# Sigmoid attention with a ReGLU layer behind it: three weight sums, two relus and two token sums change their places in the order

## The chip, the cores and the metric

The kernel runs on one core of a Trainium2 chip. The metric is the device time of one execution in microseconds (us). A core has four compute engines with an instruction stream each: TensorE (PE, with its weight loads PEld), VectorE (DVE), ScalarE (ACT) and GpSimd (POOL). SyncE (SP) and POOL issue most DMAs. Each engine works its stream in order; streams wait for each other by semaphores.

## The reference

Eight batches of 12 heads with 448 tokens of 64 channels. Attention has a sigmoid in place of the softmax; its output, 3584 tokens of 768 channels, goes through a gated layer:

```python
scores = scale * np.matmul(q, k.transpose(0, 1, 3, 2)) - np.log(S)
attn = 1.0 / (1.0 + np.exp(-scores))
x = matmul(attn, v)                      # then (batch, token, head*64)
gate = np.maximum(x @ w_gate, 0.0)       # 768 -> 1536
out = (gate * (x @ w_val)) @ w_out       # 1536 -> 768
```

Inputs and output are float32; the kernel multiplies in float16 and adds up in float32.

## The kernel before, in words

**Attention.** A batch has three groups of four heads. q and k are transposed: batches 0 and 1 on TensorE (`pe_transposes`), later ones by DMA (`dma_transposes`, L218): VectorE copies k and q into a `rel` buffer (L222, two buffers, L53), and SP issues one DMA transpose of it (L226). `qk_unit` (L299) makes the scores of one of seven key chunks of a group in two PSUM banks, and ScalarE writes their sigmoids into `PT` (L187). `pv` (L249) multiplies the seven chunks by v into two banks, which `put_xT` copies into `xT` (L184).

**PSUM.** After the first stage all eight banks are one ring: `bank` (L77) takes the one in front and puts it at the back. So each tile takes the bank of the tile eight places before it, and its first matmul waits until that tile has been read.

**The gated layer.** `gv` (L311) does one block f of 128 of the 1536 columns for some tokens: six matmuls for the gate product `g_ps`, six for the value product `v_ps`, then in `gv_out` (L331) a relu into `gate_sb` (on ScalarE, L334, if `act_relu`, otherwise on VectorE, L336) and on VectorE the product `hT` = gate times value (L343), here called the gating. The gating frees the bank of `v_ps`, the relu that of `g_ps`. For batch 0 a block is done in two halves of tokens, 256 (half 0) and 192 (half 1), called units. For batch 1 the blocks 8 to 11 are done whole (kind "u" in `work`); its other blocks and all of the later batches go by a seven-product scheme (`gv_split`, `gv_pair`), and so do most of the down products (`down_pair`, L460). Those schemes want sums of blocks, made by VectorE beforehand: `early_sum_steps` (L563: four steps for two blocks, 0 to 7, one `gate_sums` in place in wv and three S tiles), `weight_sums` (L410: the four T tiles, sums of blocks of wo) and `token_sum_steps` (L440: four sums of `hT`; only the first two are moved here).

**The order around the first edit.** It is written out by hand. In batch 1 the 21 qk units come in six stretches, `cuts` (L933): in the fourth and sixth, pv of a group stands after two qk units. After each stretch `ffn_mix` (L770) takes 4, 3, 3, 3, 3 and 4 units of batch 0 from `gv_queue`, which `push_first` has filled in the order half 0, half 1 for each pair of blocks. The fifth stretch has the units (half 0, f 9), (half 1, f 8) and (half 1, f 9). Hooks run before a unit: in the fifth stretch the k and q copies and the transpose of batch 2's group 0 before the first unit and of group 1 before the third, in the sixth `late_loads` before the first. `late_loads` (L868) does the copies and transpose of group 2, then `hold` (L861): POOL copies two numbers of that group's transposed tile, so that every POOL DMA behind it (v of batch 2, k and q of batch 3, the two loads of wo, v of batch 3) is issued after that transpose has landed. `given` (L953) says how many sum steps VectorE gets at each unit.

**The order around the second edit.** Batches 2 and on have again six stretches, each followed by one item of `work` (`next_work`, L901); `ahead` jobs run before the item, `jobs` beside it. In batch 2 the fifth stretch's item is block 10 of batch 1, the sixth's is block 11, and batch 3's first is the first down pair, `("y", 0, 0)`. `open_late` (L383) opens the T tiles and the pool of S tiles. Before the fifth item comes weight sum 0 = a difference of two quarters of wo, before the sixth weight sum 1, the first token sum and the copies of batch 3's group 2; beside it the other three token sums.

Of the kernel before, what the change touches and what calls it, by code (L numbers as in the profile page):

```python
# [18 lines left out]
def kernel(  # L19
# [170 lines left out]
    def qkT_of(b, g):  # L190
        if (b, g) not in qkT_tiles:
            qkT_tiles[(b, g)] = qkTp.tile([P, TW, P], FP16, tag="qkT", name="qkT")
        return qkT_tiles[(b, g)]
# [24 lines left out]
    def dma_transposes(b, g):  # L218
        k16, q16, _ = in_tiles[b]
        rel = relp.tile([P, TW, P], FP16, tag="rel", name="rel")  # L220
        for ti, t16 in enumerate((k16, q16)):
            nc.vector.tensor_copy(  # L222
                rel[:, ti * NCH : (ti + 1) * NCH, :].rearrange("p c (h d) -> p h c d", h=2),
                t16[:, 2 * g : 2 * g + 2, :].rearrange("p h (c d) -> p h c d", c=NCH),
            )
        nc.sync.dma_start_transpose(  # L226
            qkT_of(b, g)[:], rel[:].rearrange("p c x -> p (c x)")
        )
# [78 lines left out]
    def pv_group(b, g):  # L307
        pv(b, g, 0, S, [PT_tiles.pop((b, g, c))[:, :, 0:S] for c in range(NCH)])
# [81 lines left out]
    def sub(o, a, b):  # L390
        nc.vector.tensor_tensor(out=o, in0=a, in1=b, op=AOP.subtract)  # L391

    def sums_tile(inner):
        S3 = late["sums"].tile([P, 3, HF * P], FP16, tag="S", name="S")
        return [S3[:, i, :].rearrange("p (x y) -> p x y", y=inner) for i in range(3)]
# [14 lines left out]
    def weight_sums(i):  # L410
        T = [late["T"][:, j] for j in range(4)]
        B11, B21 = wo[:, 0:HF, 0:HM], wo[:, HF:NFC, 0:HM]
        B12, B22 = wo[:, 0:HF, HM:DM], wo[:, HF:NFC, HM:DM]
        sub(T[i], *((B12, B11), (B22, T[0]), (B22, B12), (B21, T[1]))[i])
# [14 lines left out]
    def token_blocks(g, p):  # L429
        blocks = []  # L430
        for gt, t in tiles_in(g, p):
            h = odd[gt] if gt < g else hT_tiles[g][:, :, t * P : (t + 1) * P]
            blocks += [h[:, 0:HF, :], h[:, HF:NFC, :]]
        return blocks
# [5 lines left out]
    def token_sum_steps(g, p, k0=0, k1=HF):  # L440
        if ("y", g, p) not in sums:
            sums[("y", g, p)] = sums_tile(P)
        S1, S2, S4 = (t[:, k0:k1, :] for t in sums[("y", g, p)])
        A11, A12, A21, A22 = (t[:, k0:k1, :] for t in token_blocks(g, p))
        return (
            lambda: nc.vector.tensor_tensor(out=S1, in0=A21, in1=A22, op=AOP.add),
            lambda: sub(S2, S1, A11),
            lambda: sub(S4, A12, S2),
            lambda: sub(A21, A11, A21),
        )  # L450
# [311 lines left out]
    def push_gv(b, q0, qn, fs, act_relu=True):  # L762
        for f in fs:
            gv_queue.append(lambda f=f: gv(b, q0, qn, f, act_relu))

    def push_first(half, fs, act_relu=True):
        c0, c1 = HALVES[half]
        push_gv(0, 64 * c0, 64 * (c1 - c0), fs, act_relu)

    def ffn_mix(count, hooks=(), steps=(), given=()):  # L770
        hooks = list(hooks)
        for left in range(count, -1, -1):
            while hooks and hooks[0][0] >= left:
                hooks.pop(0)[1]()
            if left:
                gv_queue.popleft()()
                for step in itertools.islice(steps, given[count - left] if steps else 0):
                    step()


    nc.scalar.activation(gate[:], zeros[:, 0:2], AF.Sigmoid, bias=sig_bias, scale=qk_scale)
# [3 lines left out]
    half = QCUT // 2 * D  # L785
# [61 lines left out]
    push_first(1, range(0, 4))  # L847
    for f0 in range(4, 12, 2):
        for half in range(2):
            push_first(half, range(f0, f0 + 2))  # L850


    order = [(g, c) for g in range(NG) for c in range(NCH)]
# [1 line left out]
    def pv_finish(b):  # L855
        pv_group(b, NG - 1)
# [7 lines left out]
    def both(b, g):  # L864
        pe_transposes(b, g, 0)
        pe_transposes(b, g, 1)
# [64 lines left out]
    for b in range(1, B):  # L931
        if b == 1:
            cuts, pv_at = (0, 3, 6, 9, 13, 17, 21), {3: (0, 2), 5: (1, 2)}  # L933
        else:
            cuts, pv_at = (0, 4, 7, 11, 14, 18, 21), {0: (-1, 2), 2: (0, 2), 4: (1, 2)}
        bursts = list(range(len(cuts) - 1))
        inner = {}
        if b > 2:
            inner = {0: 1, 3: 5} if b == 3 else {0: 1} if b % 2 == 0 else {2: 3, 3: 5} if b == B - 1 else {4: 5}
            for n in inner.values():  # L940
                bursts.remove(n)
        count = len(bursts)
        hooks = {}
        if b == 1:
            mix = (4, 3, 3, 3, 3, 4)
            hooks = {
                1: [(3, lambda: both(1, 1))],
                3: [(3, lambda: both(1, 2))],
                4: [(3, lambda: dma_transposes(2, 0)), (1, lambda: dma_transposes(2, 1))],
                5: [(4, late_loads)],  # L950
            }
            steps = itertools.chain.from_iterable(early_sum_steps(j, 2 * j) for j in range(4))
            given = ((0, 1, 1, 0), (1, 1, 0), (1, 1, 1), (1, 1, 0), (2, 1, 0), (1, 1, 1, 1))  # L953
        else:
            mix = (0,) * count

        def burst(n):
            for i, (g, c) in enumerate(order[cuts[n] : cuts[n + 1]]):
                if n in pv_at and i == pv_at[n][1]:
                    if n == 0:  # L960
                        pv_finish(b - 1)
                        if b == 2:
                            push_group(0)
                        elif b % 2 == 0:
                            push_group(b // 2 - 1)
                    else:
                        pv_group(b, pv_at[n][0])
                qk_unit(b, g, c)

        for m in range(count):  # L970
            jobs, ahead = [], []
            burst(bursts[m])
            if m == 0 and b > 3:
                jobs.append(lambda: dma_transposes(b, 2))
            if b == 2 and m == 2:
                ahead.append(lambda: dma_transposes(3, 0))
            elif b == 2 and m == 3:
                jobs.append(lambda: dma_transposes(3, 1))
            elif b == 3 and m == count - 1:
                jobs.append(lambda: dma_transposes(4, 1))  # L980
            elif 0 <= m - count + 2 and 3 < b < B - 1:
                jobs.append(lambda: dma_transposes(b + 1, m - count + 2))
            if b == 1:
                if m == 0:
                    load(2, 0, 1, "kq")
                    load(2, 1, 2, "kq")
                    load(2, 2, 3, "kq")
            elif m == 0 and b + 1 < B:
                for g0, g1 in ((0, 1), (1, NG)) if b == 3 else ((0, NG),) if b > 3 else ():
                    jobs.append(lambda g0=g0, g1=g1: load(b + 1, g0, g1, "kq"))  # L990
                jobs.append(lambda: load_v(b + 1))
            if b == 2 and m == 0:
                ahead.append(lambda: split_sums(1))
            elif b == 2 and m == 4:
                open_late()
                ahead.append(lambda: weight_sums(0))
                first_sums = token_sum_steps(0, 0)
            elif b == 2 and m == 5:
                ahead += [lambda: weight_sums(1), first_sums[0], lambda: dma_transposes(3, 2)]
                jobs += first_sums[1:]  # L1000
            elif b == 3 and m == 0:
                jobs.append(lambda: (weight_sums(2), weight_sums(3)))
            elif b == 3 and m < 3:
                jobs.append(lambda: gate_sums(6 + 2 * m, 8 + 2 * m))
            if b % 2 and b > 2:
                if m == count - 1:
                    jobs.append(lambda: (batch_sums_t1(b // 2), batch_sums(b // 2, (0, 1))))
            elif b > 3 and m == 0:
                jobs.append(lambda: batch_sums(b // 2 - 1, (1, HD)))
            if mix[m]:  # L1010
                for job in jobs:
                    job()
                ffn_mix(mix[m], hooks.get(m, ()), steps, given[m])
            else:
                next_work(
                    jobs, ahead=ahead,
                    amid=(lambda: burst(inner[m])) if m in inner else None,
                )
            if b == 3 and m == count - 2:
                dma_transposes(4, 0)  # L1020
# [35 lines left out]
```

## Time and profile before

| | |
|---|---|
| median of three runs | 390.95 us (390.76 to 391.09) |
| the profiled execution | 390.65 us |
| its span, first to last instruction | 388.9 us |
| TensorE clock granted | 1.00 |
| TensorE busy | 98% of the span |

The page gives, for each engine, busy time, its share of the span and the number of instructions. In the order of time a line has the start, the duration in us, the engine, the line, the operation with output and inputs, the shape and how many instructions are merged in it; in square brackets the idle time of the engine just before and what ended it. "issue" there means that the profile shows no engine that it waited for. A DMA line has the KB of each transfer and the time from issue to landing.

### The profile page before, as it was taken

The page shows a single profiled execution, that of the slowest core. Times are in us where ns is not written, and L with a number is a line of the kernel's source. Part 1 is how long each engine was busy: PE and PEld are TensorE (multiplying, and loading weights), DVE is VectorE, ACT ScalarE, POOL GpSimd, SP SyncE. Part 2 cuts the span into 40 slices and gives each one's busy share as a digit, 9 for nine tenths or more (in the row PEclk, how much of TensorE's full clock was granted, in tenths as well). Part 3 has the DMA queues.
Part 4 walks back from the last instruction along what each step waited for, and adds up shares of the span by engine and source line. Part 5 has one row for each costly group of instructions (what it writes and reads, how often), then busy time and mean ns, then how long its engine had stood idle before and what let it go on. Part 6 is the DMA issues. An engine that isn't in the chain of part 4 may idle for free.

```text
span 388.9 us, 8970 instructions
## 1 busy us (share of the span) xinstructions
PE 382.0 (98%) x3576; PEld 223.6 (58%) x3576; DVE 299.4 (77%) x593; ACT 227.9 (59%) x482; POOL 50.0 (13%) x73
## 2 busy tenths in 40 slices
PE   8999999999999999999999999999999999999995
PEld 6678766885555545454455554545455555555663
DVE  3455667768867799999757789999987788999563
ACT  5967777567797755555547764545477354333321
POOL 8633405300500300003000300000000000000000
PEclk9999999999999999999999999999999999999999
DMA  9999998999997990226945793222012220000335
GB/s 168 199 199 204 204 185 135 206 197 174 113 250 154 157 227 7 48 49 90 171 88 130 136 233 58 41 56 49 1 33 70 72 74 1 2 0 2 81 87 159
DMA packets 68987, 43.81 MB, mean 113 GB/s; under 512 B 35664, under 2 KB 65616, under 8 KB 68944
## 3 DMA queue, kind: packets, MB, share of 16 engines
q0 software_dynamic: 30496, 23.24, 40.2%
q1 hardware_dynamic: 37664, 19.24, 24.0%
q10 hardware_dynamic: 784, 0.75, 0.6%
q8 instruction: 28, 0.46, 0.5%
q14 instruction: 15, 0.12, 0.1%
HBM read 47.19 MB, written 11.01 MB: 150 GB/s over the span
## 4 chain that ended last, share of the span: by engine, by line
PE 93%; ACT 3%; DVE 1%; DMA 1%; issue 1%; DVEq 0%; ACTq 0%
PE u L400 34%; PE g L400 16%; PE y L400 11%; PE qk_ps L239 9%; PE pv_ps L257 8%; PE g_ps L322 5%; PE v_ps L322 4%; ACT PT L187 3%; PE u L714 2%; PE g L714 2%; PE ya L366 1%; PE trt L204 1%; PE yb L366 1%; DMA ysb<-in_k_dram 1%; DVE S L391 0%
## 5 line engine op out<-in xcount | busy, mean ns | idle before, releaser
L187 ACT ACTIVATE PT<-qk_ps 128x448 f16<-128x448 f32 (+3 forms) x318 | 151.3, 585 | 80.9 <-PE qk_ps L239 79.9
L400 PEld LDWEIGHTS <-S 128*128 128x128 f16 x558 | 54.6, 98 | 44.9 <-issue 0.3
L633 DVE TENSOR_TENSOR gsb<-g,gsb 128x448 f32<-128x448 f32 x72 | 42.8, 624 | 10.1 <-PE g L400 9.8
L239 PE MATMUL qk_ps<-qkT 64*64 64x448 f16 (+2 forms) x756 | 47.8, 336 | 0.5 <-ACT PT L187 0.3
L400 PEld LDWEIGHTS <-hT 128*128 128x128 f16 x306 | 28.5, 98 | 22.7 <-issue 5.2
L629 ACT COPY gsb<-u 128x448 f32<-128x448 f32 x48 | 25.6, 558 | 24.0 <-PE u L400 22.9
L257 PE MATMUL pv_ps<-PT,v 64*64 64x448 f16 (+2 forms) x756 | 37.3, 329 | 0.8 <-DVE hT L343 0.8
L184 DVE TENSOR_SCALAR xT<-pv_ps 128x448 f16<-128x448 f32 (+2 forms) x53 | 27.8, 565 | 9.1 <-PE pv_ps L257 7.6
L458 ACT ACTIVATE ysb<-u 128x384 f32<-128x384 f32 x30 | 14.7, 490 | 34.1 <-PE u L400 29.6
L400 PEld LDWEIGHTS <-wg 128*128 128x128 f16 x216 | 20.2, 98 | 21.8 <-issue 4.3
L400 PEld LDWEIGHTS <-wv 128*128 128x128 f16 x216 | 21.1, 98 | 19.7
L239 PEld LDWEIGHTS <-qkT 64*64 64x64 f16 x756 | 17.9, 105 | 20.9 <-issue 14.9
L476 DVE SCALAR_TENSOR_TENSOR ysb<-y,ysb 128x384 f32<-128x384 f32 x29 | 16.1, 555 | 17.9 <-PE y L400 10.4
L111 POOL DMA_DIRECT2D k<-in_k_dram x14 | 10.9, 775 | 142.0 <-DVE rel L222 135.6
L257 PEld LDWEIGHTS <-v 64*64 64x64 f16 x756 | 21.9, 107 | 11.8 <-issue 2.0
L400 PE MATMUL u<-T,hT 128*128 128x384 f16 x132 | 25.1, 327 | 0.0
L400 PE MATMUL u<-xT,wg 128*128 128x448 f16 x108 | 23.5, 354 | 0.0
L400 PE MATMUL g<-xT,wg 128*128 128x448 f16 x108 | 23.4, 352 | 0.0
L400 PE MATMUL g<-X,S 128*128 128x448 f16 x108 | 23.4, 352 | 0.0
L400 PE MATMUL u<-X,wv 128*128 128x448 f16 x108 | 23.4, 352 | 0.0
L400 PE MATMUL u<-X,S 128*128 128x448 f16 x108 | 23.4, 352 | 0.0
L400 PE MATMUL u<-xT,wv 128*128 128x448 f16 x108 | 23.4, 352 | 0.0
(94 smaller groups left out, 562.3 us busy)
## 6 DMA issues: line engine op xcount, KB each, us to landing
out_dram<-ysb SPq DMA_DIRECT2D x52, 192.0 KB, 3.0
v<-in_v_dram POOLq DMA_DIRECT2D x8, 336.0 KB, 15.5
v<-in_v_dram POOLq DMA_DIRECT2D x16, 168.0 KB, 14.9
k<-in_k_dram POOLq DMA_DIRECT2D x4, 672.0 KB, 10.8
q<-in_q_dram POOLq DMA_DIRECT2D x4, 672.0 KB, 13.8
k<-in_k_dram POOLq DMA_DIRECT2D x9, 224.0 KB, 11.7
q<-in_q_dram POOLq DMA_DIRECT2D x7, 224.0 KB, 12.4
wo<-in_moe_w_out_dram POOLq DMA_DIRECT2D x1, 1536.0 KB, 18.2
```

The costliest lines, as they stand in the source:

```text
L111: nc.gpsimd.dma_start(t16[:, xs, cs], rows_of(src, b)[:, xs, cs])
L184: nc.vector.tensor_scalar(out=xT, in0=src, scalar1=XSCALE, scalar2=None, op0=AOP.mult)
L187: nc.scalar.activation(PT_ap, ps_ap, AF.Sigmoid, bias=sig_bias, scale=qk_scale)
L239: nc.tensor.matmul(out_of(hh)[o : o + 64, :], qkT[rows, c, cols], qkT[rows, NCH + c0 : NCH + c1, cols], start=True, stop=True, tile_positi ...
L257: nc.tensor.matmul(ps[hh][64 * r : 64 * r + 64, 0:qn], v16[rows, 2 * g + hh, c * D : (c + 1) * D], pieces[c][rows, hh, :], start=(c == 0), ...
L322: nc.tensor.matmul(ps[:, 0:qn], (wg, wv)[i][:, dc, f * P : (f + 1) * P], xT_tiles[b][:, dc, q0 : q0 + qn], start=(dc == 0), stop=(dc == ND ...
L400: nc.tensor.matmul(ps[:, 0:n], A[:, k_, :], W[:, k_, :], start=(first and k_ == 0), stop=(k_ == kn - 1), skip_group_check=True,)
L458: nc.scalar.activation(o, ps[:, 0:HM], AF.Copy, scale=OUT_SCALE)
L476: nc.vector.scalar_tensor_tensor(out=o, in0=ps[:, 0:HM], scalar=OUT_SCALE, in1=o, op0=AOP.mult, op1=AOP.add)
L629: by(gs[u][i][:], ps[u][:, 0:S])
L633: nc.vector.tensor_tensor(out=gs[u][i][:], in0=ps[u][:, 0:S], in1=gs[u][i][:], op=AOP.add)
L714: nc.tensor.matmul(ps[j // 2][:, j % 2 * SQ : (j % 2 + 1) * SQ], sets[j][i][:, k_, :], W[:, k_, :], start=(first and j % 2 == 0 and k_ == ...
```

## The change

Three things in the order; nothing that is computed differs. `ffn_mix` lets the sum steps go before the unit in place of behind it, and may give steps after the last one; the table `given` is set so that one step moves from the fifth stretch to the end of the first, and the two that the fifth keeps stand ahead of all its units. The relus of (half 0, f 9) and (half 1, f 8) go to VectorE. In batch 2 the first token sum moves from the sixth item to ahead of weight sum 0, and the second from beside the sixth item to the same place.

```diff
         for left in range(count, -1, -1):
             while hooks and hooks[0][0] >= left:
                 hooks.pop(0)[1]()
+            for step in itertools.islice(steps, given[count - left] if steps else 0):
+                step()
             if left:
                 gv_queue.popleft()()
-                for step in itertools.islice(steps, given[count - left] if steps else 0):
-                    step()
...
         for half in range(2):
-            push_first(half, range(f0, f0 + 2))
+            for f in range(f0, f0 + 2):
+                push_first(half, (f,), (half, f) not in ((0, 9), (1, 8)))
...
-            given = ((0, 1, 1, 0), (1, 1, 0), (1, 1, 1), (1, 1, 0), (2, 1, 0), (1, 1, 1, 1))
+            given = ((0, 0, 1, 1, 1), (0, 1, 1, 0), (0, 1, 1, 1), (0, 1, 1, 0), (2, 0, 0, 0), (0, 1, 1, 1, 1))
...
             elif b == 2 and m == 4:
                 open_late()
-                ahead.append(lambda: weight_sums(0))
                 first_sums = token_sum_steps(0, 0)
+                ahead += [*first_sums[:2], lambda: weight_sums(0)]
             elif b == 2 and m == 5:
-                ahead += [lambda: weight_sums(1), first_sums[0], lambda: dma_transposes(3, 2)]
-                jobs += first_sums[1:]
+                ahead += [lambda: weight_sums(1), lambda: dma_transposes(3, 2)]
+                jobs += first_sums[2:]
```

## The prediction

> **What bounds the kernel.** I read the page's busy table and chain first, then TensorE's, VectorE's and ScalarE's order of time around the two edits, then the DMA issues.
>
> ```profile
> span 388.9 us, 8970 instructions
> ...
> PE 382.0 (98%) x3576; PEld 223.6 (58%) x3576; DVE 299.4 (77%) x593; ACT 227.9 (59%) x482; POOL 50.0 (13%) x73
> ...
> PE 93%; ACT 3%; DVE 1%; DMA 1%; issue 1%; DVEq 0%; ACTq 0%
> ...
> wo<-in_moe_w_out_dram POOLq DMA_DIRECT2D x1, 768.0 KB, 25.0
> ```
>
> TensorE sets the end, and its instruction order is the same in both kernels. So only holes in TensorE's stream can be won or added. TensorE at the start of the sixth stretch:
>
> ```profile
> 53.90 0.78 PE L239 MATMUL qk_ps<-qkT 64*64 64x448 f16 x8
> 54.31 0.53 PE L257 MATMUL pv_ps<-PT,v 64*64 64x448 f16 x2
> 55.62 1.51 PE L257 MATMUL pv_ps<-PT,v 64*64 64x448 f16 x26 [0.79 <-DVE hT L343]
> 56.79 0.74 PE L239 MATMUL qk_ps<-qkT 64*64 64x448 f16 x8
> 57.46 0.83 PE L322 MATMUL g_ps<-xT,wg 128*128 128x256 f16 x6
> ```
>
> The same eight qk, 28 pv and eight qk matmuls take 62.17 to 64.38 = 2.21 us one stretch later; here 53.90 to 57.46 = 3.56. The hole is 1.35 us. VectorE before it:
>
> ```profile
> 51.70 0.40 DVE L222 COPY rel<-q 128x896 f16<-128x896 f16 x1 [0.71 <-DMA q<-in_q_dram]
> 53.83 0.42 DVE L343 TENSOR_TENSOR hT<-gate_sb,v_ps 128x256 f16<-128x256 f32 x1 [1.73 <-ACT gate_sb L334]
> 54.16 0.55 DVE L391 TENSOR_TENSOR S<-wv 128x768 f16<-128x768 f16 x1
> 54.75 0.56 DVE L584 TENSOR_TENSOR S<-S,wg 128x768 f16<-128x768 f16 x1
> 55.23 0.34 DVE L343 TENSOR_TENSOR hT<-gate_sb,v_ps 128x192 f16<-128x192 f32 x1
> ```
>
> VectorE stands idle 1.73 us, because the fifth stretch's three relus sit behind eight sigmoids on ScalarE (its relus run from 53.32). Then two sums go ahead of the second gating (55.23), which frees the bank pv waits for: it ends at 55.57, pv goes on at 55.62. The second place is in batch 2's end:
>
> ```profile
> 93.17 1.36 DVE L391 TENSOR_TENSOR T<-wo 128x2304 f16<-128x2304 f16 x1 [1.06 <-issue]
> 94.45 0.61 DVE L343 TENSOR_TENSOR hT<-gate_sb,v_ps 128x448 f16<-128x448 f32 x1
> ...
> 100.45 0.54 DVE L453 TENSOR_SCALAR ysb<-u 128x384 f32<-128x384 f32 x1
> ```
>
> The first weight sum reads all of wo. The second wo load is issued at about 68.1 and lands 25.0 us later, 93.1: that is its 1.06 us wait.
>
> **The change, part by part.**
>
> Moved sums, stretches 1 to 4. One 0.55 us sum goes to the end of stretch 1, where VectorE stands idle 0.53 us before the trt copy at 34.59; a sum hands over after 0.47. Cost 0 (at most 0.05, which no bank waits for). The later places hold as many sums of 0.55 us as before.
>
> Stretch 5. VectorE now runs, from the q copy at 51.70: 0.30 to the next instruction, two sums at 0.47, relu 256 wide with its dependent gating 0.50 (24.40 to 24.92 in the earlier pair was 0.52), 0.34 to the next, relu 192 wide and gating. No 192-wide relu stands on VectorE in this trace; the 192-wide xT copy from PSUM takes 0.35, the 256-wide relu 0.42, and I take 0.35, so 0.43 with the hand-over. Second gating: 51.70 + 0.30 + 0.94 + 0.50 + 0.34 + 0.43 = 54.21, end 54.56, so pv goes on at 54.61 instead of 55.62: 1.01 us. The two k/q copies (loads landing at 52.8 and 54.0) and the third gating follow, ending at 55.4; pv ends its 1.17 us at 55.78, so the next qk pair no longer waits for the third gating (56.56 + 0.34 = 56.90 in the trace), which gives 0.19. **First term: −1.20 us**; bounds −1.35 (the whole hole) and −0.7 (q lands half a microsecond later: the new sequence hangs on it). ScalarE loses two relus (0.8 us); its sigmoids of pairs two to four follow TensorE.
>
> What is late next. The third copy pair (58.07) refills the buffer that the transpose issued at 52.19 reads, and that lands after 5.8 us, at 57.99. So this copy cannot move up. The gating behind it then comes at 58.65, but the first bank wanted from it is asked for at 61.0, so TensorE keeps its 1.20. POOL does not: its wo loads stand behind the hold (L862), which waits for the transpose of exactly this copy.
>
> ```profile
> 62.90 0.31 POOL L862 COPY gate<-qkT 1x2 f16<-1x2 f16 x1 [18.28 <-DMA qkT<-rel]
> ```
>
> So wo is issued when it was, and DMA moves 200 to 207 GB/s from 70 to 85: it does not land sooner either.
>
> The two token sums (0.55 us each, 0.59 + 0.47 to the next) go in front of the first weight sum. TensorE and VectorE arrive 1.20 earlier, xT is through at 90.9, the two sums at 92.0, and the weight sum still starts at 93.17. Hence the gating of unit 10 of batch 1 (94.45, 0.61) still ends at 95.06. Banks go round in eight: unit 11's v matmuls take the bank of unit 10's v. They start at 95.45 in the trace, 0.39 clear; 1.20 earlier would be 94.25, and they must wait to 95.10. **Second term: +0.85**. The bounds: 0 if wo came 1.20 earlier; more, if it lands later. It may: the transposes of batch 3 (issued at 79.35 and about 83.3, landing 13.4 and 14.0 us later beside wo, against 4.1 for the one at 58.8 with no load beside it) are issued 1.2 us earlier and so take DMA time ahead of wo. One transpose's share is 1.2 of 13.4, or 9% of what moved beside wo; by its bytes (128x1792 at two bytes, 0.46 MB) 41 KB, at some 170 KB per us 0.25 us. Against it stands an earlier hold of up to 0.1. I add 0.10: **+0.95**.
>
> The Trainium skill (DMA: Bandwidth & Descriptors, Queues, rings and completion order) says that each DMA engine takes turns between the queues it has work for, a packet at a time. The 13.4 us beside 4.1 agree. By it the earlier transposes can only delay wo: that is the slower rival below.
>
> Behind the weight sum. The two token sums, 1.06 us, are gone from between there and the first down pair: the sequence copies, gating 11, S4, S3, xT runs to 99.4 instead of 100.45. In the trace the down pair's first copy starts at 100.45, 1.57 us after its product starts (98.88); in the next pair it is 1.19 (116.02 to 117.21), and the third product there comes 0.97 us after the second, here 1.18 (99.87 to 101.05). That 0.2 us goes: product at 98.5, copy at 99.7, end 100.3, wanted at 100.5. **Third term: −0.20**, bounds 0 and −0.20. T3 and T4 follow the copy, 0.7 us sooner. From 105 on TensorE's waits show none, so the shift reaches the end.
>
> Sum: −1.20 + 0.95 − 0.20 = **−0.45 us**. Against the profiled execution, 390.65 (span 388.9 plus 1.75 around it), 390.20; the runs shown have the median 390.95, 0.30 above it, so I predict **390.5**.
>
> Note how it is built: as long as the weight sum waits for wo, the gain up front does not matter beyond 0.35; the result is 0.39 − 0.04 + 0.20, less whatever wo is later.
>
> **Rivals.**
>
> *wo comes with TensorE.* If the third copy goes when VectorE is free (57.1) and the hold with it, all 1.20 is kept: −1.40, 389.55. For it: 57.99 is one landing read to a tenth, and with less traffic beside it the transpose might land sooner (the later ones take 4.1); the copy at 58.07 also directly followed VectorE's own work, so nothing shows it waiting. Against: the loads beside that transpose run to 56.3 as before.
>
> *wo lands later.* One mechanism: the transposes that are issued earlier delay the transfers they pass. The second transpose (56.72 now, 55.2 then) overlaps the first, and if they share rather than queue, the first lands up to 1.3 us later, the hold and wo with it; the batch-3 ones add 0.25 or more. Each microsecond of wo is one of TensorE at unit 11. With d the delay, the time changes by d − 0.55: slower from d = 0.55, and with d = 1.5 by +0.95, 391.9. Against: transposes at 56.72 and 58.8 landed two microseconds apart, each after 4.1 to 4.2, though they overlapped.
>
> *No gain up front.* If the copy pair's q load or the two sums made the second gating as late as now (55.23), the first term would be 0, the second 0 too (0.39 clear), and −0.20 would be left: 390.75. Against: VectorE's free 1.73 us.
>
> **How the numbers follow.** Forecast 0.55 (390.5, its own range 390.15 to 390.9); wo with TensorE 0.27 (389.55); wo later 0.12 (390.95 to 391.9); no gain 0.06 (390.75). The range holds 8 in 10 with forecast and first rival: 389.4 (the 1.35 hole, all kept, and the 0.2) to 391.1. What a measurement can tell from no change is 0.2%, 0.78 us. Faster by more: 0.27 plus 0.05 of the forecast = 0.32; slower by more, d over 1.33: 0.07; within: 0.61.
>
> **What would show it.** Right: pv goes on near 54.6 and the sixth stretch's first g product starts near 56.3; the hold still runs near 62.9; the weight sum's wait shrinks little though two sums stand ahead of it; a new TensorE wait of about 0.9 us for hT before unit 11's v; the third product of the first down pair 0.97 after the second. Wrong: the hold or the weight sum a microsecond earlier, or the weight sum later than 93.7.

## The result, and the profile after

The changed kernel takes 390.08 us in the median of 17 runs (389.16 to 390.96), the kernel before 390.93 in 17 runs beside it: the ratio is 0.9979, with a 95% interval of 0.9972 to 0.9987. That is 0.85 us or 0.21% faster, a little over the 0.2% (0.78 us) that the prediction took as the least that can be told from no change. The profiled execution of the changed kernel took 390.18 us (span 388.3), that of the kernel before 390.65: 0.47 apart, less than the medians are.

First the hole at the sixth stretch. TensorE in the changed kernel:

```profile
54.26 0.57 PE L239 MATMUL qk_ps<-qkT 64*64 64x448 f16 x8
54.66 1.49 PE L257 MATMUL pv_ps<-PT,v 64*64 64x448 f16 x28
55.99 0.55 PE L239 MATMUL qk_ps<-qkT 64*64 64x448 f16 x8
56.47 0.83 PE L322 MATMUL g_ps<-xT,wg 128*128 128x256 f16 x6
```

From 54.26 to 56.47 are 2.21 us, where the kernel before took 3.56: no hole is left. (TensorE came to this place 0.36 later than in the profile of before, which matters below.) VectorE beside it:

```profile
51.56 0.39 DVE L222 COPY rel<-q 128x896 f16<-128x896 f16 x1 [0.72 <-DMA q<-in_q_dram]
51.87 0.55 DVE L584 TENSOR_TENSOR S<-S,wg 128x768 f16<-128x768 f16 x1
...
54.12 0.35 DVE L343 TENSOR_TENSOR hT<-gate_sb,v_ps 128x192 f16<-128x192 f32 x1
...
57.94 0.39 DVE L222 COPY rel<-k 128x896 f16<-128x896 f16 x1 [0.59 <-DMA qkT<-rel]
```

The two sums follow the q copy at once, the second gating starts at 54.12. And the third copy pair cannot move up with the rest: it stands waiting 0.59 us for the first transpose, and goes at 57.94. So POOL's hold is where it was (62.72, before 62.90), and wo is issued 0.2 us sooner only:

```profile
62.72 0.17 POOL L863 COPY gate<-qkT 1x2 f16<-1x2 f16 x1 [18.22 <-DMA qkT<-rel]
```

The other end of that chain, VectorE first:

```profile
91.62 0.56 DVE L391 TENSOR_TENSOR S<-S,hT 128x768 f16<-128x768 f16 x1
93.13 1.36 DVE L391 TENSOR_TENSOR T<-wo 128x2304 f16<-128x2304 f16 x1 [0.95 <-DMA wo<-in_moe_w_out_dram]
94.41 0.61 DVE L343 TENSOR_TENSOR hT<-gate_sb,v_ps 128x448 f16<-128x448 f32 x1
```

Two more sums stand ahead of the weight sum, and it still waits 0.95 us (before 1.06), now with the releaser named: the wo load. It starts at 93.13, before at 93.17. TensorE pays for that at unit 11's v:

```profile
93.31 1.31 PE L322 MATMUL g_ps<-xT,wg 128*128 128x448 f16 x6
95.07 1.29 PE L322 MATMUL v_ps<-xT,wv 128*128 128x448 f16 x6 [0.46 <-DVE hT L343]
...
99.49 1.14 PE L400 MATMUL y<-T,S 128*128 128x384 f16 x6
100.47 1.14 PE L400 MATMUL u<-T,S 128*128 128x384 f16 x6
```

The same places in the kernel before:

```profile
94.30 1.31 PE L322 MATMUL g_ps<-xT,wg 128*128 128x448 f16 x6
95.45 1.30 PE L322 MATMUL v_ps<-xT,wv 128*128 128x448 f16 x6
...
99.87 1.14 PE L400 MATMUL y<-T,S 128*128 128x384 f16 x6
101.05 1.14 PE L400 MATMUL u<-T,S 128*128 128x384 f16 x6
```

From the g product to the v product there are 1.76 us in place of 1.15: v comes 0.61 us late. The third product of the down pair comes 0.98 after the second, before 1.18: that stall is gone. And the page's list of what the last chain consists of has changed with it:

```profile
PE 83%; DMA 10%; POOL 3%; issue 1%; DVE 1%; ACT 0%; POOLq 0%; DVEq 0%; ACTq 0%
```

The DMA share was 1% before. The chain now runs through the wo load: of the 10%, 6 are that load and 3 an early load of wv.

### The profile page after: what moved, and what is told of

Its sections match the earlier page's. It is cut to its first block, busy times and chain, and to the rows that moved or that the text cites. A ratio compares the mean times of both kernels' runs of the same rounds, so it can differ in the third digit from the quotient of the medians.

```text
span 388.3 us, 8972 instructions
## 1 busy us (share of the span) xinstructions
PE 381.8 (98%) x3576; PEld 224.0 (58%) x3576; DVE 300.0 (77%) x595; ACT 227.3 (59%) x480; POOL 49.8 (13%) x73
## 4 chain that ended last, share of the span: by engine, by line
PE 83%; DMA 10%; POOL 3%; issue 1%; DVE 1%; ACT 0%; POOLq 0%; DVEq 0%; ACTq 0%
PE u L400 34%; PE g L400 16%; PE y L400 11%; PE qk_ps L239 7%; PE pv_ps L257 7%; DMA wo<-in_moe_w_out_dram 6%; PE v_ps L322 4%; DMA wv<-in_moe_w_val_dram 3%; PE g_ps L322 3%; PE ya L366 1%; POOL q L111 1%; PE yb L366 1%; PE trt L204 1%; POOL k L111 1%; POOL wg L149 0%
## 5 line engine op out<-in xcount | busy, mean ns | idle before, releaser
L400 PEld LDWEIGHTS <-hT 128*128 128x128 f16 x306 | 28.5, 98 | 22.7 <-issue 5.2
L322 PE MATMUL v_ps<-xT,wv 128*128 128x256 f16 (+2 forms) x168 | 22.8, 273 | 0.7 <-DVE hT L343 0.5
```

What stands on the lines that cost most here:

```text
L322: nc.tensor.matmul(ps[:, 0:qn], (wg, wv)[i][:, dc, f * P : (f + 1) * P], xT_tiles[b][:, dc, q0 : q0 + qn], start=(dc == 0), stop=(dc == ND ...
L400: nc.tensor.matmul(ps[:, 0:n], A[:, k_, :], W[:, k_, :], start=(first and k_ == 0), stop=(k_ == kn - 1), skip_group_check=True,)
```

## The experiments

The times are medians. Each ratio is against the kernel before, run beside it on the same chip, with its 95% interval.

**The first edit alone.** The token sums go back to their old places.

```diff
-                ahead += [*first_sums[:2], lambda: weight_sums(0)]
+                ahead.append(lambda: weight_sums(0))
...
-                ahead += [lambda: weight_sums(1), lambda: dma_transposes(3, 2)]
-                jobs += first_sums[2:]
+                ahead += [lambda: weight_sums(1), first_sums[0], lambda: dma_transposes(3, 2)]
+                jobs += first_sums[1:]
```

> The first edit alone: sums ahead of the units and the two relus on VectorE, the token sums where they were. Theory (the first weight sum waits for wo, whose landing does not move): pv goes on without a hole at the sixth stretch, TensorE is over a microsecond early until unit 11's v, which waits for unit 10's gating until about 95.1; behind the weight sum stands the old sequence of VectorE, so the first down pair's copy comes at 100.4 and its third product at 101.0, where it is in the kernel before. All of the gain is given back: 0.0 us against the kernel before (-0.3 to +0.2). Rival (wo comes with TensorE): -1.2 us. Rival (the two edits each bring their part of the 0.85): -0.5 us or more.

Measured: 390.75 against 391.05, ratio 0.9985 (0.9976 to 0.9993), −0.30 us, the edge of what was expected; eight of its eleven runs lie between 390.54 and 390.89. The other three took 389.58 to 389.99, near the 389.55 that this edit takes where wo is in time (below); no trace of such a run is kept, so whether wo came early in them is open. In its profile TensorE's stretch is whole again (54.23 to 56.44) and the v product waits as in the changed kernel; then VectorE, with the sums behind the weight sum:

```profile
93.13 1.36 DVE L391 TENSOR_TENSOR T<-wo 128x2304 f16<-128x2304 f16 x1 [2.04 <-issue]
...
100.40 0.55 DVE L453 TENSOR_SCALAR ysb<-u 128x384 f32<-128x384 f32 x1
```

The weight sum now waits 2.04 us, the copy comes at 100.40, and TensorE goes on with the third product at 101.00, where the kernel before had it (101.05). In this profile the gain of the first edit is given back, all but 0.05 us, at two places within ten microseconds.

**The second edit alone.** The first edit's three hunks undone.

```diff
-            for step in itertools.islice(steps, given[count - left] if steps else 0):
-                step()
             if left:
                 gv_queue.popleft()()
+                for step in itertools.islice(steps, given[count - left] if steps else 0):
+                    step()
...
-                push_first(half, (f,), (half, f) not in ((0, 9), (1, 8)))
+                push_first(half, (f,))
...
-            given = ((0, 0, 1, 1, 1), (0, 1, 1, 0), (0, 1, 1, 1), (0, 1, 1, 0), (2, 0, 0, 0), (0, 1, 1, 1, 1))
+            given = ((0, 1, 1, 0), (1, 1, 0), (1, 1, 1), (1, 1, 0), (2, 1, 0), (1, 1, 1, 1))
```

> The second edit alone: two token sums ahead of the first weight sum, the fifth stretch as before. Theory: the sums fill 1.06 us in which VectorE waits for wo, the weight sum starts at 93.2 as before, and only the late copy of the first down pair is mended: -0.2 us. No wait before unit 11's v, which starts at 95.45. Rival (the token sums are what brings the measured gain): -0.6 to -0.9 us. Rival (they delay the weight sum): +0.1 us or more.

Measured: 390.86 against 391.05, ratio 0.9995 (0.9986 to 1.0004), −0.19 us: as the theory has it, though the interval reaches to no change. The profile shows the third product 0.98 after the second, and no wait before unit 11's v. The two edits alone make 0.49 us together, both at once 0.85: the second is not worth much by itself, it takes away the second of the two places where the first loses its gain.

**wo by rows.** In the changed kernel the two loads of wo carry the upper and lower half of its rows. The first weight sum reads the upper half only.

```diff
-        for m0, m1 in ((0, 512), (512, DM)):
+        for c0, c1 in ((0, NFC // 2), (NFC // 2, NFC)):
             nc.gpsimd.dma_start(
-                wo[:, :, m0:m1], moe_w_out[:, m0:m1].rearrange("(c p) m -> p c m", p=P)
+                wo[:, c0:c1, :], moe_w_out[c0 * P : c1 * P].rearrange("(c p) m -> p c m", p=P)
             )
```

> The changed kernel, with wo loaded as two halves of its rows instead of two column ranges, so that the first weight sum (which reads the upper rows alone) waits only for the first load. Theory: the weight sum goes at about 92.0, right behind the token sums, unit 11's v does not wait, and the whole hole of the sixth stretch is kept: -1.4 us against the kernel before (-1.2 to -1.6), and the runs of it scatter as little as those of the kernel before (some 0.6 us from end to end) and not as those of the changed kernel (1.8). Rival (something else than wo holds unit 11 back): no more than the changed kernel's -0.85 us.

Measured: 389.57 against 391.05, ratio 0.9964 (0.9951 to 0.9976), −1.48 us, the size that the theory gave. VectorE and TensorE of this kernel:

```profile
91.46 0.56 DVE L391 TENSOR_TENSOR S<-S,hT 128x768 f16<-128x768 f16 x1
91.93 1.35 DVE L391 TENSOR_TENSOR T<-wo 128x2304 f16<-128x2304 f16 x1
```

```profile
93.15 1.31 PE L322 MATMUL g_ps<-xT,wg 128*128 128x448 f16 x6
94.29 1.30 PE L322 MATMUL v_ps<-xT,wv 128*128 128x448 f16 x6
```

No wait on either. The first load lands 15.9 us after its issue, at 82.5, the second after 22.7, at 90.1, 3 us before wo was whole by columns. Both are there before the weight sum starts at 91.93, so the wait would be gone even if the sum waited for both: that the half which it reads came first is not shown to matter here, the earlier landing of the whole is enough. Its five runs lie within 0.40 us, but the 27 runs of the kernel before beside it lay within 1.30 in place of 0.61, so what the scatter shows is not settled.

**wo by rows in the kernel before.** The same edit of the loads alone.

> The kernel before, with wo loaded as two halves of its rows. Theory: the weight sum no longer waits 1.06 us, which only mends the late copy of the first down pair: -0.2 us; the hole at the sixth stretch stays 1.35 us. Rival (wo's landing is what the end hangs on also without the change): -0.8 us or more.

Measured: 391.06 against 391.05, ratio 1.0003 (0.9994 to 1.0012): no change that can be told. The rival is out; of the expected 0.2 the medians show nothing, though the interval just reaches it. The profile, of the slowest of the eleven runs, shows what can stand against it:

```profile
93.33 1.35 DVE L391 TENSOR_TENSOR T<-wo 128x2304 f16<-128x2304 f16 x1
...
98.53 0.62 DVE L343 TENSOR_TENSOR hT<-gate_sb,v_ps 128x448 f16<-128x448 f32 x1 [0.48 <-ACT gate_sb L334]
```

The weight sum waits no more, yet the gating of unit 11 waits for its relu (TensorE started 1.3 us later in this run), and three sums and xT follow before the copy. So the copy of the first down pair was late for two reasons, wo and the token sum behind unit 11's gating; here the third product comes 1.09 after the second, half mended.

**Each half of the first edit.** On the changed kernel with wo by rows, so that none of the gain is swallowed later: first with the relus back on ScalarE, then with the sums back in their places.

```diff
-                push_first(half, (f,), (half, f) not in ((0, 9), (1, 8)))
+                push_first(half, (f,))
```

> wo by rows, and of the first edit only the new places of the sums: both relus stay on ScalarE behind its eight sigmoids. Theory: the first gating still comes at 53.83, but no sum stands between it and the second, which ends at 54.51 instead of 55.57; pv goes on at 54.6 and 0.25 us of the hole is left: -1.15 us against the kernel before, 0.25 behind wo by rows with both. Rival (the relus are what fills the hole, since VectorE's 1.73 us of idle time are a wait for them): -0.3 us.

The other kernel has the old `ffn_mix` and the old `given` (the first and the last hunk of the diff shown under the second edit alone), with the relus on VectorE:

> wo by rows, and of the first edit only the two relus on VectorE: the sums stand in their old places behind the units, two between the two gatings. Theory: the first gating comes at 52.5, the two sums behind it, the second gating ends at 54.56 as with both parts, and only the third gating, with one sum more ahead of it, ends 0.47 later, 0.1 behind pv: -1.3 us against the kernel before. Rival (the sums between the gatings are the cause): -0.5 us or less.

Measured: the sums alone 389.83 against 390.95, ratio 0.9970 (0.9958 to 0.9982), −1.12; the relus alone 389.66, ratio 0.9966 (0.9954 to 0.9978), −1.29. Both as the theory said, and both rivals fall: either half closes most of the hole. By the profiles the stretch from the first qk to the first g takes 2.50 us with the sums alone (54.25 to 56.75), 2.23 with the relus alone (55.45 to 57.68), 3.56 with neither. The second gating in the two, sums first:

```profile
54.19 0.69 DVE L343 TENSOR_TENSOR hT<-gate_sb,v_ps 128x256 f16<-128x256 f32 x2 [1.59 <-ACT gate_sb L334]
```

```profile
53.92 0.55 DVE L391 TENSOR_TENSOR S<-wv 128x768 f16<-128x768 f16 x1
...
55.44 0.35 DVE L343 TENSOR_TENSOR hT<-gate_sb,v_ps 128x192 f16<-128x192 f32 x1
```

With the relus on ScalarE VectorE still stands idle for 1.59 us, and it costs little, since both gatings then follow each other. With the relus on VectorE the sums may stand between the gatings, since the first comes early. The hole needed both: late relus and two sums behind the first of them.

**The first edit with wo by rows.** As the first experiment, with wo by rows.

> wo by rows and the first edit, the token sums in their old places. Theory: with wo out of the way the weight sum starts at 91.9 and unit 11's v does not wait; the second token sum stands again behind unit 11's gating and the down pair's copy is 0.1 us late, as in the kernel before with wo by rows: -1.3 us against the kernel before, 0.1 to 0.2 behind wo by rows with both edits. Rival (the token sums bring more than that by themselves): -1.0 us or less.

Measured: 389.55 against 390.95, ratio 0.9964 (0.9952 to 0.9976), −1.40. Without the wait for wo the first edit alone brings what both bring, as near as these runs tell; the profile has the third product 1.09 after the second, 0.1 late, as expected.

**The hold moved to group 1.** wo by columns as in the changed kernel, but issued sooner.

```diff
-        hold(2, 2)
+        hold(2, 1)
```

> The changed kernel, wo by columns as there, but POOL's hold waits for the transpose of group 1 instead of group 2, so that the loads behind it, wo's among them, are issued some 3 us earlier, partly beside the transpose of group 2. Theory (the changed kernel's end is set by when wo is issued and lands): wo lands 1.5 to 3 us earlier, the weight sum no longer waits, unit 11's v neither, -1.4 us against the kernel before and the small scatter of wo by rows. Rival (the DMA engines are full and the transpose takes from wo what the earlier issue gives): the weight sum still waits to about 93, no more than the changed kernel's -0.85.

Measured: 389.73 against 390.95, ratio 0.9963 (0.9951 to 0.9975), −1.22. The hold runs at 59.54 in place of 62.72, wo is whole at about 90.9 in place of 93.1, the weight sum starts at 92.05 right behind the token sum of 91.57, and unit 11's v follows its g after 1.15. As near as these runs tell it is the same gain, by another way of getting wo earlier: it is the time at which wo is there, not the shape of its load.

**TensorE made late.** Six matmuls of 256 columns repeated ahead of one g product in the third stretch, in the kernel before and in the changed one.

```diff
         ps = bank(("g_ps", "v_ps")[i])
+        for _ in range(6 if (b, q0, f, i) == (0, 0, 6, 0) else 0):
+            nc.tensor.matmul(
+                ps[:, 0:qn], wg[:, 0, f * P : (f + 1) * P], xT_tiles[b][:, 0, q0 : q0 + qn],
+                start=True, stop=True,
+            )
```

> The kernel before, with six matmuls of 256 columns repeated ahead of one g product of stretch 3 (overwritten by it): TensorE comes some 0.65 us later to the sixth stretch, nothing is asked of the DMA queues. Theory (here TensorE's own work sets the end, with 0.39 us clear at unit 11's v, and the late copy of the first down pair, which hangs on wo, is met 0.65 later): +0.45 to +0.65 us. Rival (lateness on TensorE is hidden anyway, also here): 0.0.

> The changed kernel with the same six matmuls. Theory (its end is set by wo's landing, and TensorE stands about 0.5 to 0.9 us waiting before unit 11's v): the 0.65 us are taken out of that wait, and the time is that of the changed kernel, within 0.2 us of -0.85 against the kernel before. That is why the kernel before, whose early stretches start later in most runs than in its profile, loses by this and the changed kernel does not. Rival (the end is not pinned; the changed kernel is only shorter): -0.2 us against the kernel before.

Measured: the kernel before 391.72 against 391.10, ratio 1.0015 (1.0005 to 1.0026), +0.62; the changed kernel 390.32, ratio 0.9977 (0.9969 to 0.9986), −0.78, where the change without the matmuls had 0.9979. What costs the one 0.62 us is hidden in the other. The rows say the same. In the kernel before the fifth stretch starts at 50.56 (49.49 without the matmuls), in the changed kernel at 50.62 (49.86 without); the third product of the down pair follows in the two, the kernel before first:

```profile
102.04 1.14 PE L405 MATMUL u<-T,S 128*128 128x384 f16 x6
```

```profile
100.61 1.14 PE L405 MATMUL u<-T,S 128*128 128x384 f16 x6
```

So 1.07 us late at the fifth stretch are still 0.99 there in the kernel before (101.05 without), and 0.76 are 0.14 in the changed one (100.47). In this profile of the changed kernel the weight sum starts at 92.85, straight behind the token sum of 92.38: the wait is gone. TensorE's lateness alone would have left some 0.3 us of it; wo was also whole some 0.7 us sooner, 24.4 us after its issue in place of 25.2.

**v of batch 3 ahead of wo.** In the changed kernel.

```diff
         load(3, 0, NG, "kq")
+        load_v(3)
         load_o()
...
-                jobs.append(lambda: load_v(b + 1))
+                if b > 2:
+                    jobs.append(lambda: load_v(b + 1))
```

> The changed kernel, with batch 3's v loaded ahead of wo in the same queue instead of behind it: 672 KB at some 200 KB per us, so wo is through about 3 us later. Theory: the first weight sum starts near 96.3, unit 11's v waits to about 98.2, and the time is 3 us over that of the changed kernel, 2.2 us over the kernel before (1.7 to 2.8): a microsecond of wo for a microsecond of the end. Rival (wo's landing is only a part of it): less than 1 us over the changed kernel.

Measured: 396.61 against 391.10, ratio 1.0136 (1.0120 to 1.0152), +5.51 us, which is 6.4 over the changed kernel (−0.85): twice what was expected. VectorE and TensorE:

```profile
97.26 1.36 DVE L391 TENSOR_TENSOR T<-wo 128x2304 f16<-128x2304 f16 x1 [5.14 <-DMA wo<-in_moe_w_out_dram]
```

```profile
99.20 2.40 PE L322 MATMUL v_ps<-xT,wv 128*128 128x448 f16 x6 [4.65 <-DVE hT L343]
...
102.28 2.83 PE L257 MATMUL pv_ps<-PT,v 64*64 64x448 f16 x28
...
105.43 1.15 PE L400 MATMUL u<-wo,hT 128*128 128x384 f16 x6
```

wo came 4.1 us later, not 3 (weight sum 97.26 against 93.13), and v starts 4.13 later: a microsecond for a microsecond, as the theory has it. Then the six v matmuls take 2.40 us in place of 1.29 and pv 2.83 in place of 1.49, and the down pair starts 6.92 later. The other 2.8 us, which the expectation did not have, are the clock; see the last section.

## Why the prediction was right, and where it was off

The mechanism was right in each of its main steps; the size was 0.45 against 0.85 measured: 390.08 is in the whole range and just below the forecast's own, 390.15 to 390.9. It lies on the side of 0.2% to which I gave 0.32, against 0.61 for no change that can be told.

- *Moved sums in stretches 1 to 4, cost 0.* Right: the changed kernel's stretches from the third to the fifth stand at the same distances (38.95, 43.36, 49.86 against 38.58, 42.99, 49.49: 0.37 each time). The 0.37 are there before any sum has moved, at the first stretch (28.88 against 28.51), and 0.27 of them are a wait for a load of wv at 23.56.
- *First term, −1.20.* The steps of VectorE came as worked out: gating 54.12 for 54.21 forecast. In the changed kernel's profile all of the 1.35 is gone, since TensorE came 0.37 later while the q load did not. The kernel with the moved hold, where TensorE came at the same time as in the profile of before (49.52 against 49.49), shows 53.92 to 56.42 = 2.50 us: 1.06 us saved, 0.14 less than forecast. The missing part is in the second pair of qk, 0.72 where 0.55 is usual; it is most of the 0.19 that the first term counted on there. The third gating, which I had named for it, had ended at 55.42, before the pair starts (55.77). The profile names no wait: the eight matmuls, which the changed kernel starts four at a time (55.99 and 56.18), start in smaller lots up to 56.14. Why they do so is open.
- *Third copy pair pinned to the first transpose, hold and wo unmoved.* Right: 0.59 us of waiting, hold 62.72, weight sum 93.13 for 93.17 forecast, unit 11's v at 95.07 for 95.10. TensorE waits there 0.61 us in place of the 0.85 of the second term, because in this execution it came 0.99 us earlier than in the profile of before and not 1.20. The prediction says that the weight sum reads all of wo; it reads two quarters, the upper half of the rows, and by columns each of the two loads carries a part of them, so the wait is the same. The landing of wo took 25.2 us from its issue at 67.9 in place of 25.0 from 68.1: the earlier hold and the longer flight together gave −0.04, where I had put +0.10.
- *The Trainium skill's rule that each DMA engine takes turns between its queues* (DMA: Bandwidth & Descriptors, Queues, rings and completion order). The 0.2 us that wo's flight grew is no more than the change's earlier transposes could take by it. Six profiles have wo by columns behind the hold as it was: the flight is 25.2 us in the two where the first transpose of batch 3 is issued 10.5 us behind the second wo load, and 24.4 to 25.0 in the four where it is 11.1 to 11.3. The direction agrees with the rule; the four differ among themselves by more than the 0.2, so the size is not shown.
- *Third term, −0.20.* Right, 0.98 for 1.18. The experiments add that the stall had two causes.
- *No gain up front* and *wo later* did not happen. *wo with TensorE* did not happen either, as the hold shows; the two kernels in which wo is early show what it would have been worth, 389.6 to 389.7, or −1.48 and −1.22 for the −1.40 worked out.
- **The step that was off** is the last of the sum: "the runs shown have the median 390.95, 0.30 above it, so I predict 390.5". On the profiled executions the sum was 390.20 and 390.18 was measured, a nearness that is in part luck: from the third product of the down pair to the last product of the kernel the rows stand 0.58 us earlier, the −0.45 and the 0.14 by which wo came sooner than assumed, and some 0.1 us of that was lost again outside the span. The 0.30 was carried over as if any execution were later than the profile by the same amount in both kernels. But what makes TensorE late ahead of the sixth stretch costs the kernel before its full length, and in the changed kernel it goes into the wait for wo. TensorE made 0.65 us late shows it: +0.62 in one, nothing that can be measured in the other. That ordinary executions are late there is likely, not shown: all ten other profiles without the added matmuls start the fifth stretch later than the profile of before (49.52 to 51.05, against 49.49), and four of them name the load of wv as what TensorE waited for. One of them, the kernel before with wo by rows, starts it 1.30 us later and took 391.98, 0.92 over the median of its runs. Without the 0.30 the forecast would have been 390.2. Open is why the changed kernel's runs lie 1.80 us apart, those of the kernel before 0.61: the lowest, 389.16 to 389.49, are where the kernels with wo in time are, and a flight of wo that varies as it does in the profiles (24.4 to 25.2) could do it, but none of these runs has a trace.

## What to carry to other kernels

Before counting a stall that is taken out up front, look for the next place where the path waits for something that does not move with it, a load held back by a chain of its own, and how much it is clear there (0.39 us here): no more than that is kept. A profile is one execution; where two streams meet, differences between executions are worth nothing in the one that waits and everything in the one that is waited for, so they may not be carried over from one kernel to the other. And the two mends of the wait, loading wo by rows and issuing it sooner, have one thing in common: all of wo was there, at 90.1 and about 90.9, before VectorE asked for it. Ask first what sets the time at which a load is whole; that the waiting sum reads only half of wo gave the idea, but is not shown to have been needed.

## What the runs showed of the hardware

The clock of TensorE fell after one long wait. In the kernel with v ahead of wo, TensorE stood 4.65 us; the profile's windows (PE busy, PEld, DVE, ACT, POOL, then the granted clock, DMA share and GB/s):

```profile
94.00:99.00 5.00, 0.55 (x3) 0.20 (x2) 1.74 (x2) 2.14 (x5) 0.00 (x0) 0.92 0.91 117
99.00:102.00 3.00, 2.80 (x14) 0.97 (x17) 2.32 (x5) 0.00 (x0) 0.82 (x2) 0.50 0.00 0
102.00:105.40 3.40, 3.40 (x44) 1.52 (x36) 1.52 (x4) 1.85 (x4) 2.10 (x3) 0.56 1.39 128
105.40:110.00 4.60, 4.60 (x40) 2.53 (x36) 4.28 (x6) 2.91 (x7) 1.99 (x3) 1.00 0.97 130
```

The granted clock was 0.50 and 0.56 up to about 105 and 1.00 behind it; at the low clock the v matmuls and pv took 2.40 and 2.83 us in place of 1.29 and 1.49, most of the 2.8 us. By the means of the windows (0.92 in the first, 0.56 in the third) the clock fell near 98.2, during the wait itself, and came back near 105.0. The 0.46 us wait in the changed kernel left it at 1.00. The Trainium skill (TensorE: Matmul & The Clock Gate, Part 1: The HAM clock gate) states that the clock halves after an idle window of about 3.4 us and comes back after as long a busy one. The fall agrees with it, some 3.6 us after the last matmul before the wait ended. The clock was back some 6 us after the work began again, 6.8 after it fell: longer than one such window counted from either.
